# Pooled attention and MLP in one kernel: the first group's first product in blocks of 128 tokens, and the second group's loads in smaller pieces around the weights

One core of one Trainium2 chip runs the kernel. The metric is device time in microseconds (us) of that core, the median of several executions.

## The reference

```python
# q, k, v: (8, 8, 576, 64) f32;  moe_w_in: (512, 2048) f32;  moe_w_out: (2048, 512) f32
k_p = k.reshape(B, H, 72, 8, 64).mean(axis=3)          # pooling of 8 rows
v_p = v.reshape(B, H, 72, 8, 64).mean(axis=3)
attn = softmax(q @ k_p.transpose(0, 1, 3, 2) / 8)      # 576 x 72 for each head
x = (attn @ v_p).transpose(0, 2, 1, 3).reshape(4608, 512)
out = gelu_tanh(x @ moe_w_in) @ moe_w_out              # 4608 x 512, f32
```

## The kernel before

The kernel works on groups of 512 tokens. Groups 0 to 7 hold the first 512 tokens of each batch; a ninth group, R, holds the 64 tokens that are left of each, and is worked between groups 6 and 7. While TensorE does the MLP of one group, the other engines prepare the attention of the next one. Functions put into `hooks` at step s are called just before matmul s of the MLP, so the program order of every engine is written by hand.

For every group the normalised attention weights `eb` are transposed to `eT`. For group 0 TensorE does that; for all others the DMA does it (`e_transpose_dma`, four per group, issued from SyncE), and the values products, which start the next group, read `eT`.

```python
def e_transpose_dma(g, j):
    nc.sync.dma_start_transpose(out=st[g]["eT"][:, j], in_=eb[:, j])

def hidden_half(g, fo, half, hook, s):                 # first product of group 0: 256 tokens at a time
    c0 = 256 * half
    hp = psum.tile([128, 2, 256], F32, name="mm", tag="mm", bufs=4)
    for f in range(2):
        for ko in range(KO):
            hook(s + 4 * f + ko)
            nc.tensor.matmul(out=hp[:, f, :], lhsT=w_in_b[:, ko, (fo + f) * 128:(fo + f + 1) * 128],
                             rhs=st[g]["xT"][:, ko, c0:c0 + 256], start=(ko == 0), stop=(ko == KO - 1))
    nc.scalar.activation(out=gT[:, fo:fo + 2, c0:c0 + 256], in_=hp, func=ACT.Gelu_apprx_tanh)
# ... cut
def warm_up(n, tag):                                   # called with 12, ahead of the work
    warm = psum.tile([128, MAIN], F32, name="warm", tag=tag, bufs=BUFS[tag])
    for _ in range(n):
        nc.tensor.matmul(out=warm, lhsT=zeros, rhs=zeros.unsqueeze(1).to_broadcast([128, 4, 128]),
                         start=True, stop=True)
# ... cut: the loads of group 0 and of w_in stand ahead of these, all on SyncE's queue
load_main(1, "k", 0, 4, nc.sync)
load_half(1, "k", nc.sync)
load_half(1, "v", nc.sync)
load_q(1, 0, 4, nc.sync)
for c in range(4):
    w_out_load(c)                                      # 1 MB each
load_main(1, "v", 0, 2, nc.sync)
load_main(1, "v", 2, 4, nc.sync)
# ... cut: hooks of group 1's attention in group 0's MLP (second product from step 128 on)
for j in range(4):
    at(hooks, [128, 131, 142, 146][j], scores, 1, j)
    at(hooks, [128, 131, 142, 146][j], exps, 1, j)
    at(hooks, [142, 146, 150, 154][j], norm, 1, j, nc.vector)
    at(hooks, [142, 146, 150, 154][j], e_transpose_dma, 1, j)
for f in range(8, 16, 2):
    at(hooks, 147, cast_w_out, f, f + 2, nc.scalar)
# ... cut
tail_of_attention(hooks, 1, 186)                       # values of group 1
```

The softmax here doesn't subtract the row's maximum and nothing guards it: scores larger than these inputs give would overflow.

## Time and profile before

| | before |
|---|---|
| device time, median of 3 (lowest to highest) | 294.52 us (294.45 to 294.75) |
| span in the profile | 292.6 us |
| TensorE busy | 97% |
| first hidden matmul of group 0 | 17.43 us |
| first output matmul of group 0 | 35.71 us |
| values of group 1, start and end | 49.07 and 50.86 us |
| transposes of `eT` for group 1 landed | 46.44, 47.01, 47.58, 48.18 us |

The span is the profiled execution from its first to its last instruction; the device time is about 2 us longer. The lines of the page, of the stretches, of TensorE's timeline and of the chain stand in the prediction below.

### The profile page before, as it was taken

Reading aid. Unit: us, or ns where it says so; the run is one execution under the profiler, and the core shown is the slowest. Engines: PE = TensorE matmul, PEld = TensorE weight load, DVE = VectorE, ACT = ScalarE, POOL = GpSimd, SP = SyncE. Lnnn points to the kernel's source line nnn. Section 1 sums busy time; section 2 is a strip of 40 time slices with the busy share of each in tenths; the row PEclk is TensorE's granted clock in tenths of the full one; section 3 lists DMA queues with packets and bytes.
Section 4 is the critical chain, followed back from the end, with each engine's and each line's share of the span. In section 5 each row is a group of like instructions: output and inputs, shape, how many; then the busy total and the mean of one; then the engine's idle time right before and its main releaser. Section 6 shows DMA issues by size and latency. Waiting matters only on the chain.

```text
span 292.6 us, 4562 instructions
## 1 busy us (share of the span) xinstructions
PE 284.2 (97%) x1712; PEld 142.8 (49%) x1739; DVE 141.8 (48%) x236; ACT 156.4 (53%) x233; POOL 64.7 (22%) x86
## 2 busy tenths in 40 slices
PE   8899999999999999999999999999999999999996
PEld 3678753445444544454445444544444544444444
DVE  5892778076517460757065806481639100920012
ACT  1586574777067706671567257724673377436500
POOL 4575443222303040114002400240024000100000
PEclk9999999999999999999999999999999999999999
DMA  7999999996699369945994599148944900451012
GB/s 234 354 386 347 380 381 201 340 257 168 149 298 278 102 134 288 251 142 133 268 283 150 126 250 299 15 113 243 293 146 103 183 23 2 85 112 38 0 72 72
DMA packets 73301, 56.32 MB, mean 192 GB/s; under 512 B 45888, under 2 KB 55488, under 8 KB 73280
## 3 DMA queue, kind: packets, MB, share of 16 engines
q1 hardware_dynamic: 73136, 55.98, 69.6%
q8 instruction: 13, 0.21, 0.3%
q10 hardware_dynamic: 144, 0.07, 0.1%
q14 instruction: 8, 0.07, 0.1%
HBM read 36.70 MB, written 9.44 MB: 158 GB/s over the span
## 4 chain that ended last, share of the span: by engine, by line
PE 81%; DMA 8%; DVE 4%; SPq 3%; ACT 1%; issue 1%; POOL 0%; ACTq 0%
PE mm L360 37%; PE mm L344 36%; DMA w_out_s<-in_moe_w_out_dram 5%; DMA w_in_s<-in_moe_w_in_dram 3%; PE xo L310 3%; PE sc L214 2%; SPq L437 2%; DVE eb L248 1%; ACT gT L346 1%; PE mm L388 1%; DVE den L236 1%; SPq L99 1%; PE xo L319 1%; DVE kv L132 0%; DVE kv L133 0%
## 5 line engine op out<-in xcount | busy, mean ns | idle before, releaser
L360 PE MATMUL mm<-w_out_b,gT 128*128 128x512 bf16 x543 | 125.9, 379 | 1.4 <-issue 0.8
L344 PE MATMUL mm<-xT,w_in_b 128*128 128x512 bf16 x502 | 111.4, 379 | 0.5
L346 ACT ACTIVATE gT<-mm 128x512 bf16<-128x512 f32 x128 | 76.4, 597 | 38.4 <-PE mm L344 38.4
L360 PEld LDWEIGHTS <-gT 128*128 128x128 bf16 x560 | 53.1, 98 | 60.3 <-issue 3.1
L344 PEld LDWEIGHTS <-w_in_b 128*128 128x128 bf16 x512 | 50.1, 98 | 60.5 <-issue 0.3
L81 DVE COPY osb<-mm 128x512 f32<-128x512 f32 (+2 forms) x37 | 24.2, 657 | 58.9 <-PE mm L360 52.8
L79 ACT CAST xT<-xo 128x1024 bf16<-128x1024 f32 (+1 forms) x18 | 16.6, 967 | 56.6 <-PE xo L310 48.2
L154 POOL TENSOR_TENSOR vbd<-kvb,vmask 128x256 bf16<-128x256 bf16 (+2 forms) x40 | 21.5, 561 | 105.1 <-DVE kvb L134 104.9
L236 DVE TENSOR_REDUCE den<-e 128x8 f32<-128x576 f32 x36 | 26.5, 736 | 36.8 <-ACT e L229 36.8
L132 DVE TENSOR_TENSOR kv<-kv 128x1024 f32<-128x1024 f32 (+3 forms) x19 | 21.8, 1149 | 38.4 <-DMA kv<-in_v_dram 32.3
L229 ACT ACTIVATE e<-sc 128x576 f32<-128x576 f32 x36 | 22.4, 650 | 9.6 <-ACT e L229 4.1
L248 DVE TENSOR_TENSOR eb<-e,r 128x576 bf16<-128x576 f32 x24 | 23.3, 972 | 0.8
L81 POOL CAST q_b<-q_sb 128x2048 bf16<-128x2048 f32 (+2 forms) x9 | 17.4, 1937 | 14.5 <-DMA q_sb<-in_q_dram 14.5
L248 POOL TENSOR_TENSOR eb<-e,r 128x576 bf16<-128x576 f32 x6 | 6.9, 1150 | 57.3 <-ACT e L229 30.4
L355 PE MATMUL mm<-xT,w_in_b 128*128 128x256 bf16 x128 | 15.5, 273 | 0.2 <-DVE xT L81 0.2
L214 PE MATMUL sc<-kbd,qT 128*128 128x144 bf16 x128 | 13.3, 226 | 0.4 <-ACT qT L79 0.2
L214 PEld LDWEIGHTS <-qT 128*128 128x128 bf16 x128 | 9.9, 98 | 7.3 <-issue 0.7
L355 PEld LDWEIGHTS <-w_in_b 128*128 128x128 bf16 x128 | 12.1, 98 | 1.8 <-issue 0.3
L133 DVE TENSOR_TENSOR kv<-kv 128x512 f32<-128x512 f32 (+3 forms) x19 | 12.4, 651 | 0.7
L357 ACT ACTIVATE gT<-mm 128x512 bf16<-128x512 f32 x16 | 9.5, 597 | 5.9 <-PE mm L355 5.8
L558 ACT ACT_TABLE_LOAD x8 | 10.3, 1283 | 0.1
L81 POOL CAST w_in_b<-w_in_s 128x512 bf16<-128x512 f32 (+1 forms) x10 | 8.6, 874 | 2.4 <-DMA w_in_s<-in_moe_w_in_dram 2.4
(62 smaller groups left out, 123.5 us busy)
## 6 DMA issues: line engine op xcount, KB each, us to landing
out_dram<-osb SPq DMA_DIRECT2D x31, 256.0 KB, 6.8
kv<-in_k_dram SPq DMA_DIRECT2D x7, 1024.0 KB, 7.6
q_sb<-in_q_dram SPq DMA_DIRECT2D x7, 1024.0 KB, 6.2
kv<-in_v_dram SPq DMA_DIRECT2D x6, 1024.0 KB, 9.2
w_in_s<-in_moe_w_in_dram SPq DMA_DIRECT2D x8, 512.0 KB, 9.8
w_out_s<-in_moe_w_out_dram SPq DMA_DIRECT2D x4, 1024.0 KB, 13.7
kv<-in_v_dram SPq DMA_DIRECT2D x4, 512.0 KB, 10.2
out_dram<-osb SPq DMA_DIRECT2D x9, 128.0 KB, 2.4
```

The costliest lines, as they stand in the source:

```text
L79: eng.copy(out=out, in_=in_)
L81: eng.tensor_copy(out=out, in_=in_)
L132: add(out=t[:, :, 0:4, :], in0=t[:, :, 0:4, :], in1=t[:, :, 4:8, :], op=ALU.add)
L154: eng.tensor_tensor(out=vbd[p0:128, b, n0:n1, :].rearrange("p (c r) (hh d) -> p c (r hh) d", c=max(m, 1), d=D), in0=kvb[p0:128, 4 + c0:4 + ...
L214: nc.tensor.matmul(out=o, lhsT=qT[:, j, pr, :], rhs=kbd[:, g, pr].rearrange("d hh s -> d (hh s)"), start=True, stop=True)
L229: nc.scalar.activation(out=e.rearrange("p (x h) s -> p x (h s)", x=2), in_=sc[:, :, 0:4 * Sp], func=ACT.Exp, scale=1.0 / 64.0)
L236: nc.vector.reduce_sum(out=den, in_=e, axis=AX.X)
L248: eng.tensor_tensor(out=o.rearrange("p (h s) -> p h s", s=Sp), in0=e, in1=r.unsqueeze(2).to_broadcast([128, H, Sp]), op=ALU.mult)
L344: nc.tensor.matmul(out=hp, lhsT=w_in_b[:, ko, fo * 128:(fo + 1) * 128], rhs=st[g]["xT"][:, ko, :], start=(i == 0), stop=(i == KO - 1))
L346: nc.scalar.activation(out=gT[:, fo, :], in_=hp, func=ACT.Gelu_apprx_tanh)
L355: nc.tensor.matmul(out=hp[:, f, :], lhsT=w_in_b[:, ko, (fo + f) * 128:(fo + f + 1) * 128], rhs=st[g]["xT"][:, ko, c0:c0 + 256], start=(ko ...
L360: nc.tensor.matmul(out=o, lhsT=gT[:, fo, r * 128:(r + 1) * 128], rhs=w_out_b[:, fo, :], start=(fo == 0), stop=(fo == FO - 1))
```

## The change

The intent is to start TensorE's dense work earlier. Block 0 of 128 tokens can enter the first product as soon as its own attention is done; more weights are then used per token, so w_in is needed in another order. The loads of group 1 are cut into smaller pieces and moved around the weights: half of k goes ahead of w_in's last quarter, q comes in two loads, w_out's first MB in two, and half of v goes ahead of w_out's last MB. Two of the four norms of group 1 give three heads to ScalarE.

```diff
-    def hidden_half(g, fo, half, hook, s):
+    def hidden_block(g, c, j, hook, s):
-        hp = psum.tile([128, 2, 256], F32, name="mm", tag="mm", bufs=4)
-        for f in range(2):
+        hp = psum.tile([128, 4, 128], F32, name="mm", tag="mm", bufs=4)
+        for f in range(4):
+            fo = 4 * c + f
             for ko in range(KO):
...
-        for half, c in [(0, 0), (0, 1), (0, 2), (1, 0), (0, 3), (1, 1), (1, 2), (1, 3)]:
-            for fo in range(4 * c, 4 * c + 4, 2):
-                hidden_half(g, fo, half, hook, s)
-                s += 8
+        for c, j in [(0, 0), (0, 1), (1, 0), (1, 1), (0, 2), (1, 2), (0, 3), (1, 3)] + [(c, j) for c in (2, 3) for j in range(4)]:
+            hidden_block(g, c, j, hook, s)
+            s += 16
...   (w_in's loads)
+        if c == 3:
+            kv_tile(1)
+            load_main(1, "k", 0, 2, nc.sync)
...   (w_out's loads)
+        step = 2 if c == 0 else 4
+        for f in range(4 * c, 4 * c + 4, step):
...
-    load_main(1, "k", 0, 4, nc.sync)
+    load_main(1, "k", 2, 4, nc.sync)
     load_half(1, "k", nc.sync)
     load_half(1, "v", nc.sync)
-    load_q(1, 0, 4, nc.sync)
+    load_q(1, 0, 2, nc.sync)
+    load_q(1, 2, 4, nc.sync)
     for c in range(4):
+        if c == 3:
+            load_main(1, "v", 0, 2, nc.sync)
         w_out_load(c)
-    load_main(1, "v", 0, 2, nc.sync)
     load_main(1, "v", 2, 4, nc.sync)
...   (hooks of group 1; the second product now starts at step 256)
+    for f in range(8, 12, 2):
+        at(hooks, 275, cast_w_out, f, f + 2, nc.scalar)
+    for j in range(2):
+        at(hooks, 275, norm, 1, j, nc.vector)
+        at(hooks, 275, e_transpose_dma, 1, j)
+    at(hooks, 276, norm_two, 1, 2, 5)
+    at(hooks, 276, e_transpose_dma, 1, 2)
+    at(hooks, 277, cast_w_out, 12, 13, nc.scalar)
+    at(hooks, 277, norm_two, 1, 3, 5)
+    at(hooks, 277, e_transpose_dma, 1, 3)
+    for f0, f1 in [(13, 14), (14, 16)]:
+        at(hooks, 278, cast_w_out, f0, f1, nc.scalar)
```

Cut from the diff: `values_half` becomes `values_block` in the same way, the attention of group 0 is put in another order, and the remaining hooks move to the new step numbers.

## The prediction

> **What bounds the kernel now.** I read the page first, then busy time by stretches, then the timeline of TensorE from 14 to 53 us, and last the chain of waits up to 52 us. The page:
>
> ```profile
> span 292.6 us, 4562 instructions
> PE 284.2 (97%) x1712; PEld 142.8 (49%) x1739; DVE 141.8 (48%) x236; ACT 156.4 (53%) x233; POOL 64.7 (22%) x86
> PE   8899999999999999999999999999999999999996
> DMA  7999999996699369945994599148944900451012
> ```
>
> TensorE is busy 97% of the span at full clock; only the first two slices (15 us) are below 9 tenths. DMA is full from about 2 to 45 us and has room after that. By stretches (start of the first MLP product, start and end of what follows until the values of group 1 are done):
>
> ```profile
> 0.00:17.43 17.43, 14.43 (x100) 9.05 (x101) 12.65 (x26) 7.79 (x17) 8.79 (x23) 1.00 0.96 309
> 17.43:35.71 18.28, 17.71 (x171) 14.92 (x171) 11.62 (x25) 11.82 (x20) 9.61 (x12) 1.00 1.06 368
> 35.71:50.86 15.15, 14.97 (x85) 6.86 (x87) 11.65 (x20) 9.32 (x12) 6.96 (x9) 1.00 1.03 294
> 50.86:292.61 241.75, 237.06 (x1358) 112.00 (x1382) 105.85 (x166) 127.51 (x187) 39.31 (x44) 1.00 0.63 164
> ```
>
> Columns: stretch, length, busy time of PE, PEld, DVE, ACT, POOL, clock, DMA share, GB/s. The last row, 241.75 us, is seven and a half groups of dense matmuls that the diff leaves alone. All that can move is in the first 50.86 us. TensorE there:
>
> ```profile
> 16.81 0.41 PE L214 MATMUL sc<-kbd,qT 128*128 128x144 bf16 x4
> 17.43 1.91 PE L355 MATMUL mm<-xT,w_in_b 128*128 128x256 bf16 x16 [0.21 <-DVE xT L81]
> 19.75 1.47 PE L355 MATMUL mm<-xT,w_in_b 128*128 128x256 bf16 x12
> 23.06 9.01 PE L355 MATMUL mm<-xT,w_in_b 128*128 128x256 bf16 x81
> 49.07 1.79 PE L310 MATMUL xo<-eT,vbd 32*64 32x512 bf16 x16
> ```
>
> The first hidden product waits for the values' copy (DVE xT). From 23.06 on it runs solid. The values of group 1 take 1.79 us, where the same 16 take 1.18 us at 259 us: 0.6 us of waiting. The chain of waits says what stands behind both ends:
>
> ```profile
> 11.40 9.91 DMA w_in_s<-in_moe_w_in_dram
> 21.31 13.68 DMA w_out_s<-in_moe_w_out_dram
> 35.04 0.63 POOL w_out_b L81
> 45.45 0.61 DVE kv L132
> 48.88 0.62 POOL vbd L154
> 49.55 1.31 PE xo L310 x13
> ```
>
> The start of the second product hangs on w_out's first MB, which lands at 34.99 us. The end of the stretch hangs on VectorE (the norms of group 1 from 37.94, then the pooling of v) and GpSimd's spread. So the stage is bound by three things that lie within a microsecond of one another: TensorE's work, the order of the loads, and VectorE's chain. That is the reason to expect little.
>
> **What the Trainium skill says.** (1) "TensorE: Matmul & The Clock Gate", Back-to-back issue gap, gives about 81 ns for a 128-column matmul with its own weight load in a stream, against some 56 ns isolated. This decides what blocks of 128 cost, and the trace disagrees with 81: the 81 matmuls at 23.06 give (9.01-0.27)/80 = 109.2 ns for 256 columns; the last product has 16 of 256 and 32 of 128 columns in 3.55 us of the chain, so (3.55-16*0.1092)/32 = 56.3 ns; and 64 values of 64 columns, each with its own weight load, take 2.03 us, under 32 ns each. I use 56.3. (2) "SBUF — State Buffer", Who interferes with whom: a VectorE copy in two-port mode and GpSimd block each other for a whole instruction. The trace agrees: the same 512-element cast of w_in took VectorE 0.87 us while GpSimd was casting and 0.41 us without. (3) "DMA: Bandwidth & Descriptors", Why small descriptors are slow: a fixed cost per packet. The trace agrees: by its landings, 512 KB of v, in long rows, take 1.37 us (two loads, 8.65 to 11.40), and the halves of q, in 512-byte rows, 1.77 us (6.89 to 8.65 and 11.40 to 13.18); q of group 1 as one MB takes 2.75 us (29.55 to 32.30).
>
> **The change, part by part.**
> (a) Values and hidden in blocks of 128. The hidden matmuls go from 128 of 256 columns (128*109.2 = 13.98 us) to 256 of 128 (256*56.3 = 14.41): +0.43 us on TensorE, on the path. Values go from 16*109.2 = 1.75 to 32*56.3 = 1.80: nothing. The gelus stay 16 of 128x512. The copies of values become eight of half the size: off the path but for the first.
> (b) The start. Block 0 needs only the weights of token block 0. ScalarE loses the norm_two pieces of block 1 (3*0.28 us), so its copy of eT can start near 13.8 instead of 14.97. Values of block 0 then run at about 14.5 and, with the last spread of v near 15.2, at 15.3. Block 1's values stand before the hidden product in program order and need eT of block 1 (VectorE, near 15.9). w_in's first two loads land at 14.53 and 15.89 and their casts take 0.6 to 1.0 us, the second one behind the lock. So hidden starts near 16.8 instead of 17.43: -0.6 us.
> (c) What lies in the hidden stretch. Work after the change: 14.41 + scores of block 3 (0.25) + 10 transposes of e (0.57) + values of blocks 2 and 3 (16*0.0563 = 0.9) + transposes of k (0.28) and of q (16*0.057 = 0.91) = 17.3 us. Before: 13.98 + 0.57 + 0.87 + 0.28 + 0.91 = 16.6 us in 17.43 to 35.15, so 1.1 us idle. After the change the third block (quarter 1 of w_in) wants its weights near 19.1 and 19.6. The quarter's second half lands at 18.60, and before the casts behind it ended at 20.44; with less lock 19.9 to 20.4. I take 0.6 us of wait here. End of hidden: 16.8 + 17.3 + 0.6 = 34.7, against 35.15: -0.45 us.
> (d) The loads. Half of k (1.36 us) goes ahead of w_in's last quarter. It then lands near 26.6 instead of 25.2; it is wanted after 30, so free. w_out's first MB in two pieces: its first half would land 1.36 us before 34.99, but q in two loads of 512-byte rows costs 2*1.77-2.75 = +0.8 us ahead of it, so about 34.4. With a cast of 0.63 the second product can start at about 35.1 instead of 35.71: -0.6 us. The second half of q lands near 33.1 and its GpSimd cast (1.04 to 1.54 us) ends 34.2 to 34.6, just when its transposes are due: up to 0.4 us of wait, within the same limit of 35.1.
> (e) The end of the stretch. Norms of group 1: 2*1.7 + 2*1.47 (ScalarE takes three heads of two of them) instead of 4*1.7 = -0.46 us on the chain. Half of v ahead of w_out's last quarter lets its pooling start without waiting. But v's last half lands no earlier, since the same bytes stand ahead of it (45.74 before, about 46.5 with (d)), and the DMA transposes of e queue behind it: their last landing was 48.18, after it about 48.9. Pooling the last half ends near 48.0, spread to 48.7. So the values start near 49.0 and run without most of their 0.6 us of waiting: end near 50.2 instead of 50.86.
> Sum, at the end of the stretch: -0.6 us. After it nothing changes: 294.52 - 0.6 = **293.9 us**. The terms (b) and (d) don't add: each limit is passed in turn, and the last one, (e), sets what is left.
>
> **The rivals.** *One: narrow matmuls cost more than 56 ns* in a run of 256 beside a full DMA. At the skill's 81 ns, hidden would take 256*0.081 = 20.7 us, +6.8 us against 13.98, less the 0.6 of (b): about 300.5 us, slower by 2%. Against it: the 56.3 and 32 ns above. For it: those came late, when DMA was idle; but bursts of 8 transposes at 14.32, at full DMA, took 0.62 us, or 57 ns each without the 0.17 us of drain. I give this 3%. *Two: waits for w_in, q or w_out take the place of what is removed*, all of it: 294.5 to 295.3. For it: DMA is full until 44 us, the same bytes come in more pieces, and (c) lands on a cast. 25%. *Three: the loads don't pay for q's smaller rows, and VectorE with ScalarE lets the values start by 48.5*: then the start's 0.6, the shorter norms and the stall of the values all count, minus 0.4 for narrow matmuls: -1.3 to -1.7, 292.8 to 293.2. For it: the order of hooks was evidently placed to meet the loads. 20%.
>
> **Range and chances.** The middle case is 293.9. The range goes from rival three (292.8) to rival two with a bit more stall (295.3). Faster by 2% needs -5.9 us; all idle time of TensorE in the first 51 us is 17.43-14.43 + 18.28-17.71 + 15.15-14.97 = 3.8 us, so that is out of reach: 1%. Slower by 2% needs rival one: 3%. Within 2%: 96%.
>
> **What would show it.** Right: a 128-column hidden matmul every 56 ns in its long run; first hidden near 16.8; a gap near 19.5 to 20.3 before quarter 1's second half, released by GpSimd's w_in cast; the first output matmul near 35.1, released by the w_out cast; the group's values ending near 50.2; 241.7 us from there to the end. Wrong: a pitch well over 60 ns (rival one); first outputs at 35.7 or later or values after 50.9 (rival two); output from 34.5 or earlier and values done by 49.5 (rival three); any change of more than 0.5 us after the values of group 1, which I hold to be none.

## More of the kernel before

One line is in the page's list of DMA queues (packets, MB, share of the 16 engines' time):

```profile
q8 instruction: 13, 0.21, 0.3%
```

By the trace, each of these 13 packets has 16,384 bytes, and they come as TensorE works through its program. The Trainium skill, "Runtime: NRT & Kernel Launch", section Instruction fetch mechanics, explains them: instructions are streamed from memory in 16 KiB blocks of 256, by a DMA queue of the sequencer's own, and it says of the cost that it is "mostly hidden". The trace agrees with the block: on average 247 recorded TensorE instructions lie between two packets (187 to 292; a matmul counts as two, with its weight load, and some records are missing).

## The result and the profile after

The changed kernel takes 296.96 us (296.78 to 297.28) against 294.52, and both sit at full clock. The ratio is 1.0083, with a 95% interval of 1.0065 to 1.0100. Ratios here are the mean time of one kernel's fast runs over that of the other's in the same rounds, so they are not quite the ratio of the medians. Executions over 1.5% slower than the fastest of the same kernel are left out of the means. The result is correct. It is a small loss where a small gain was predicted (range 292.8 to 295.3 us).

The page of the kernel after, first line, busy times, and the queue of instruction fetches:

```profile
span 294.8 us, 4860 instructions
PE 284.2 (96%) x1856; PEld 145.2 (49%) x1883; DVE 142.0 (48%) x241; ACT 157.9 (54%) x240; POOL 65.1 (22%) x90
...
q8 instruction: 15, 0.25, 0.4%
```

TensorE is busy for the same 284.2 us; all of the 2.2 us are idle time. It has 144 more matmuls, and two more fetches. By stretches, with the same columns and the same borders as in the prediction:

```profile
0.00:16.57 16.57, 13.85 (x105) 8.87 (x105) 12.19 (x25) 7.23 (x15) 8.77 (x23) 1.00 0.95 306
16.57:35.38 18.81, 18.25 (x314) 17.47 (x312) 13.11 (x31) 11.87 (x22) 9.79 (x14) 1.00 1.07 343
35.38:52.33 16.95, 14.99 (x88) 6.71 (x88) 11.53 (x21) 11.33 (x19) 7.38 (x11) 1.00 1.11 291
52.33:294.83 242.50, 237.09 (x1357) 112.17 (x1382) 105.13 (x166) 127.48 (x187) 39.20 (x44) 1.00 0.63 165
```

The first stretch is 0.86 us shorter, as intended (16.57 against 17.43). The second gives 0.53 of that back. The third is 1.80 us longer, 16.95 against 15.15, with the same busy time. The last is 0.75 us longer, 242.50 against 241.75, although the diff touches nothing there. TensorE's timeline (start, length, what ran, and in brackets how long it had waited and for whom):

```profile
16.57 0.39 PE L355 MATMUL mm<-xT,w_in_b 128*128 128x128 bf16 x4
...
23.40 8.20 PE L355 MATMUL mm<-xT,w_in_b 128*128 128x128 bf16 x144
...
35.38 0.81 PE L360 MATMUL mm<-w_out_b,gT 128*128 128x512 bf16 x3
...
40.09 6.94 PE L360 MATMUL mm<-w_out_b,gT 128*128 128x512 bf16 x30
47.37 0.38 PE L360 MATMUL mm<-w_out_b,gT 128*128 128x512 bf16 x1 [0.34 <-ACT w_out_b L79]
48.32 1.89 PE L360 MATMUL mm<-w_out_b,gT 128*128 128x512 bf16 x8 [0.57 <-ACT w_out_b L79]
51.15 1.18 PE L310 MATMUL xo<-eT,vbd 32*64 32x512 bf16 x16 [0.94 <-DMA eT<-eb]
```

In the kernel before, the 39 output matmuls that here begin at 40.09 ran through without a wait:

```profile
40.34 8.80 PE L360 MATMUL mm<-w_out_b,gT 128*128 128x512 bf16 x39
```

So the sum for group 1, end of the values, can be taken from the two timelines. The 39 matmuls begin 0.25 us earlier. They take 1.32 us longer, from 40.09 to 50.21 = 10.12 us against 8.80, because they wait twice for ScalarE's cast of w_out (0.34 and 0.57, together 0.91); the other 0.41 us goes at the two restarts. Then TensorE waits 0.94 us for the DMA transposes; before, the values followed the matmuls at once (49.07 against 40.34 + 8.80 = 49.14, overlapping by 0.07), so this is +1.01. The values take 1.18 instead of 1.79 us, as predicted, which is -0.61. Together: -0.25 + 1.32 + 1.01 - 0.61 = +1.47 us, which is the 52.33 against 50.86.

The chain of waits of the kernel after, up to there (start, length, what):

```profile
32.46 12.96 DMA w_out_s<-in_moe_w_out_dram
...
45.97 0.84 ACT eb L266 x3
...
46.84 4.22 DMA eT<-eb
51.15 1.18 PE xo L310 x16
```

The chain runs from w_out's last MB, which lands at 45.42, through ScalarE (its cast stands ahead of the last three heads of block 3), to the last transpose, and that transpose takes 4.22 us to land. It no longer goes through VectorE and GpSimd. The transposes of group 1 landed at 47.43, 49.38, 50.62 and 51.06. Between the first two lie 1.95 us, where before there were 0.57. What the DMA engines did in the microsecond after 47.0 is in the DMA view of that window, in 40 slices of 0.025 us (GB/s of each, and the fetch):

```profile
GB/s 276 307 287 287 307 276 287 297 205 154 297 266 257 208 943 266 256 267 287 266 276 256 276 266 276 276 276 276 266 256 287 276 184 20 20 20 0 0 0 0
...
q8 instruction: 1, 0.02, 6.8%
```

A block of TensorE's instructions is fetched at 47.4 us (the slice with 943). Some 0.45 us later, at 47.83, the rate falls to nothing, with three transposes still to land, and stays there until about 49.0. The packets that start in the window from 47.75 to 49.00 take long (their time is 1.58 of the window on each of the 16 engines, the column before the last), and 20 GB/s are moved:

```profile
47.75:49.00 1.25, 0.68 (x4) 0.32 (x4) 1.01 (x3) 1.23 (x2) 0.56 (x2) 1.00 1.58 20
```

The same view of the kernel before, 44 to 49 us in slices of 0.125, has no fetch, and the data of its transposes move without a break from 45.6 (slice 14) to 47.6:

```profile
GB/s 170 121 88 82 66 82 51 84 51 51 37 35 115 265 291 293 295 256 267 285 291 283 242 228 256 231 207 219 138 33 0 0 25 25 16 0 16 16 41 131
```

Something of the same kind happens in group R. From the view of `eT` between 215 and 236 us, before:

```profile
DMA to landing us min/median/max: 2.5/2.6/2.6
```

and after, where a fetch comes at 226.2:

```profile
DMA to landing us min/median/max: 2.6/3.2/4.6
```

From the first product of group 6 to that of R are 31.00 us after (202.92 to 233.92) and 30.48 before (201.57 to 232.05): +0.52. From the first product of group 7 to the end are 31.07 against 30.73, +0.34. All groups between lie within 0.12 us of before. So 1.47 - 0.12 + 0.52 + 0.34 = 2.21 us, which is the difference of the spans.

Why does the fetch fall there? The change adds 128 + 16 matmuls to TensorE's program, with their weight loads 288 instructions. That is one block of 256 and 32 more, so every later fetch comes 32 instructions earlier, some 3.5 us in the output phase, where two instructions take 0.216 us (7 more matmuls in 1.89 - 0.38 us at 48.32). For the fetch beside group R's transposes the trace has it so: 226.21 - 202.92 = 23.29 us after the first product of group 6, against 228.14 - 201.57 = 26.57 before. I had counted the matmuls' time, and not their place in memory.

### The profile page after: what moved, and what is told of

Its sections match the earlier page's. It is cut to its first block, busy times and chain, and to the rows that moved or that the text cites. A ratio compares the mean times of both kernels' runs of the same rounds, so it can differ in the third digit from the quotient of the medians.

```text
span 294.8 us, 4860 instructions
## 1 busy us (share of the span) xinstructions
PE 284.2 (96%) x1856; PEld 145.2 (49%) x1883; DVE 142.0 (48%) x241; ACT 157.9 (54%) x240; POOL 65.1 (22%) x90
## 4 chain that ended last, share of the span: by engine, by line
PE 80%; DMA 13%; SPq 3%; ACT 2%; issue 1%; POOL 1%; DVE 0%; ACTq 0%; POOLq 0%
PE mm L344 36%; PE mm L360 36%; DMA w_out_s<-in_moe_w_out_dram 4%; DMA w_in_s<-in_moe_w_in_dram 4%; PE xo L310 3%; DMA kv<-in_v_dram 2%; DMA eT<-eb 2%; PE sc L214 2%; ACT gT L346 1%; PE mm L388 1%; SPq L454 1%; SPq L99 1%; POOL w_in_b L81 1%; PE vp L141 1%; PE xo L319 1%
## 5 line engine op out<-in xcount | busy, mean ns | idle before, releaser
L344 PEld LDWEIGHTS <-w_in_b 128*128 128x128 bf16 x512 | 50.1, 98 | 60.6 <-issue 0.3
L79 ACT CAST xT<-xo 128x1024 bf16<-128x1024 f32 (+1 forms) x21 | 17.3, 861 | 55.1 <-PE xo L310 46.6
L132 DVE TENSOR_TENSOR kv<-kv 128x512 f32<-128x512 f32 (+3 forms) x20 | 22.3, 1114 | 35.1 <-DMA kv<-in_v_dram 31.7
L81 POOL CAST q_b<-q_sb 128x2048 bf16<-128x2048 f32 (+2 forms) x9 | 16.5, 1833 | 15.5 <-DMA q_sb<-in_q_dram 15.5
L355 PE MATMUL mm<-xT,w_in_b 128*128 128x128 bf16 x256 | 16.4, 219 | 0.0
L355 PEld LDWEIGHTS <-w_in_b 128*128 128x128 bf16 x256 | 14.7, 98 | 0.3
L133 DVE TENSOR_TENSOR kv<-kv 128x256 f32<-128x256 f32 (+3 forms) x20 | 12.5, 626 | 0.7
```

The costliest lines, as they stand in the source:

```text
L79: eng.copy(out=out, in_=in_)
L81: eng.tensor_copy(out=out, in_=in_)
L132: add(out=t[:, :, 0:4, :], in0=t[:, :, 0:4, :], in1=t[:, :, 4:8, :], op=ALU.add)
L344: nc.tensor.matmul(out=hp, lhsT=w_in_b[:, ko, fo * 128:(fo + 1) * 128], rhs=st[g]["xT"][:, ko, :], start=(i == 0), stop=(i == KO - 1))
L355: nc.tensor.matmul(out=hp[:, f, :], lhsT=w_in_b[:, ko, fo * 128:(fo + 1) * 128], rhs=st[g]["xT"][:, ko, 128 * j:128 * j + 128], start=(ko ...
```

## The experiments

Three theories stand against each other. **Fetch (F):** the loss is made by the place of the instruction fetches among the DMA transposes, which a pure shift of the program would undo. **Loads (L):** the loss is made by the order and the pieces of the loads, which bring w_out's last MB and v's last half later. **Narrow matmuls (N):** 256 small ones cost time by themselves, in a way that the busy time does not show. The expectations may name the theories in other words.

### A first look, with four kernels

The first four were run on one chip (before: 294.93 us there). Two shift TensorE's program without touching anything else, by another form of the warm-up matmuls: about the same columns (6188 and 4992, against 6144) in more and narrower matmuls.

```diff
-    def warm_up(n, tag):
+    def warm_up(n, tag, c=512):
...
+            if c == 512:
...
+            else:
+                nc.tensor.matmul(out=warm[:, 0:c], lhsT=zeros, rhs=zeros[:, 0:c], start=True, stop=True)
...
-    warm_up(12, "mm")
+    warm_up(119, "mm", 52)      # s1, on the kernel after: +214 instructions
+    warm_up(39, "mm", 128)      # s2, on the kernel before: +54 instructions
```

> The changed kernel with nothing altered but its warm-up: 119 matmuls of 52 columns instead of 12 of 512 (about the same columns), so that every later TensorE instruction stands 214 places further back. Theory F (instruction fetch): the 16 KB block of TensorE instructions that was fetched at 47.4 us, in the middle of the four DMA transposes of e of group 1, is now fetched after about 52 us; the transposes land by about 49.5 instead of 51.06, the values of group 1 start at about 50.2 instead of 51.15, and the kernel takes 295.5 to 296.2 instead of 296.96. Theory L (order of loads and ScalarE's queue alone): nothing in the work, the loads or the queues has changed, so 296.8 to 297.1 and values at about 51.1.

Measured: 296.63 us, 1.0054 (1.0035 to 1.0074). The shift moved a fetch to 8.2 us, where the first loads of v were held up (the second landed at 11.26 instead of 9.91), and TensorE was at half clock from 12.6 to 16.0 us. The dense work started 2.6 us later than after. From TensorE's timeline:

```profile
19.15 0.39 PE L355 MATMUL mm<-xT,w_in_b 128*128 128x128 bf16 x4
...
53.21 2.03 PE L344 MATMUL mm<-xT,w_in_b 128*128 128x512 bf16 x8
```

Yet group 1's first product began at 53.21, earlier than the 53.57 of after: the last transpose landed at 50.34 instead of 51.06, with 0.57 us between the first two, and the values did not wait. Two things follow. The start of group 0 hardly sets the end of this stretch: 2.6 us later, TensorE came to the values only 0.5 us after the last transpose (42.01 + 8.85 = 50.86 by its timeline), so the 0.86 us won there are worth little by themselves. And with the fetch away from the transposes the wait for `eT` was gone. The expected time was missed by 0.4 us: in group 2 a wait for the keys had appeared, 0.61 us at 68.59, which after does not have (see k1 and the section on all traces).

> The kernel before with 39 warm-up matmuls of 128 columns instead of 12 of 512: later TensorE instructions stand 54 places further back. Theory F: its fetch of 52.3 us comes at about 46.5 us, in the middle of the transposes of e (45.5 to 48.2), which then land 1 to 1.5 us later; values of group 1 start 0.4 to 1.3 us later, and the kernel takes 294.9 to 296.0. Theory L: same as before, 294.3 to 294.8.

Measured: 295.01 us, 1.0000 (0.9985 to 1.0016). A fetch now came at 46.5 us, and the transposes of the kernel before landed at 46.72, 48.82, 49.38 and 49.94, the last one 1.76 us later than in before. So a fetch can delay the transposes with no other change. TensorE, itself 0.5 us later than in before (40.86 + 8.80 = 49.66), then waited for them:

```profile
50.08 1.18 PE L310 MATMUL xo<-eT,vbd 32*64 32x512 bf16 x16 [0.42 <-DMA eT<-eb]
```

The values then ran without their stall (1.18 us instead of 1.79), and group 1's first product began at 52.50 instead of 52.10. The median did not move. So the delay of the transposes and a wait of 0.42 us are shown; that they cost time as a whole is not, in the kernel before.

```diff
     for c in range(4):                                  # e1, on the kernel after
-        if c == 3:
-            load_main(1, "v", 0, 2, nc.sync)
         w_out_load(c)
+    load_main(1, "v", 0, 2, nc.sync)
     load_main(1, "v", 2, 4, nc.sync)
```

> The changed kernel with the last quarter of w_out loaded ahead of the first half of v again, as before. Theory L: w_out's quarter lands at about 44.0 instead of 45.42, ScalarE's cast of it no longer holds up its three heads of block 3, TensorE no longer waits for w_out (0.9 us at 47.4 and 48.3), the last transpose of e is issued near 45.3 instead of 46.84, and the kernel takes 295.3 to 296.0. Theory F: the fetch at 47.4 still falls among the transposes, so most of the loss stays: 296.4 to 297.

Measured: 297.95 us (296.46 to 299.12), 1.0095 (1.0070 to 1.0120). The edit did what it should at first: w_out's last MB landed at 44.19, and TensorE never waited for it. But the fetch still came at 47.4, the last transpose landed at 51.34, and TensorE, which was now early, stood idle for 2.37 us. One limit had taken the place of another. And the gap cost more than its length. The windows of this run from 50 us on (the column after the five busy times is the clock):

```profile
50.00:51.00 1.00, 0.00 (x0) 0.00 (x0) 0.25 (x1) 0.00 (x0) 0.10 (x1) 1.00 0.88 196
51.00:52.00 1.00, 0.57 (x8) 0.22 (x8) 0.00 (x0) 0.00 (x0) 0.00 (x0) 0.63 1.09 318
52.00:53.00 1.00, 1.00 (x16) 0.19 (x8) 0.00 (x0) 0.00 (x0) 0.00 (x0) 0.50 1.09 347
...
54.00:55.00 1.00, 1.00 (x5) 0.34 (x3) 0.50 (x1) 1.00 (x2) 0.53 (x1) 0.66 1.06 387
```

The granted clock fell to half for about 3.4 us. Four of the six executions had a mean clock of 0.994 and took 297.77 to 299.12 us; the two near full clock took 296.46 and 296.82. So the fall costs some 1.7 us when it comes (the means of the four and of the two are 298.36 and 296.64). The Trainium skill, "TensorE: Matmul & The Clock Gate", gives in its section What's actually happening a window of about 3.4 us for both directions, and advises in Why this matters for your kernels against gaps of more than some 3 us. The length of the low clock agrees; the safe gap does not, since here the fall came with a gap of 2.37 us.

```diff
     at(hooks, 276, e_transpose_dma, 1, 2)               # e2, on the kernel after
-    at(hooks, 277, cast_w_out, 12, 13, nc.scalar)
     at(hooks, 277, norm_two, 1, 3, 5)
     at(hooks, 277, e_transpose_dma, 1, 3)
+    at(hooks, 277, cast_w_out, 12, 13, nc.scalar)
```

> The changed kernel with ScalarE's three heads of block 3 ahead of its first cast of w_out's last quarter. Theory L: block 3 of e is ready near 45.0 instead of 46.81, its transpose is issued near 45.1; but TensorE still waits for w_out, even 0.5 us more if the cast is moved behind: values near 50.2 to 50.6, kernel 296.0 to 296.6. Theory F: with the transposes done earlier by 1.5 us less of them is left when the fetch comes at 47.4, so it would help too, to the same 296.0 to 296.6; only the landing times tell.

Measured: 297.17 us, 1.0080 (1.0057 to 1.0104). Block 3 was normalised earlier, but the last transpose was still issued at 46.79: SyncE was held in the issue of the third transpose from 44.27 on, for 2.41 us, to shortly before v's last half landed (46.95). So the order on ScalarE, which the chain of waits names, is not what holds the transposes. The expectation was wrong. TensorE waited 1.86 us for `eT`, and the clock fell to half here too, from 52.85 to 56.26.

### Work and loads taken apart

One chip again (before: 294.85 us).

```diff
-    warm_up(12, "mm")           # f1, on the kernel after: s2's shift of 54 instructions
+    warm_up(39, "mm", 128)
```

> The changed kernel with 39 warm-up matmuls of 128 columns instead of 12 of 512 (54 more TensorE instructions ahead, and none of the early trouble that the shift by 214 brought, where a fetch fell on the first loads of v). Theory F: the fetch of 47.4 us comes near 42, while w_out and v load; the last transpose of e lands at 49.4 to 49.9 instead of 51.06, the values of group 1 start at 50.2, the second group's first product at 52.6 instead of 53.57, and the time falls by about 1 us against the changed kernel (ratio to before 1.004 to 1.006). If the fetch alone is not it: ratio 1.008 as in the first comparison.

Measured: 296.32 us, 1.0044 (1.0028 to 1.0060). The fetch came at 43.8 us, ahead of the transposes, and they landed at 48.20, 48.76, 50.00 and 50.43. The view of `eT` from 38 to 53 us has these times from issue to landing, for after and then for f1:

```profile
DMA to landing us min/median/max: 4.2/6.9/7.3
```

```profile
DMA to landing us min/median/max: 2.8/5.7/7.1
```

TensorE did not wait for them (no bracket), in f1:

```profile
50.90 1.18 PE L310 MATMUL xo<-eT,vbd 32*64 32x512 bf16 x16
```

In group R the loss was gone too: 202.97 to 233.44 are 30.47 us, as in before. The loads came 0.8 us later (v's last half at 47.62), so not all of it arrived in the time. Nor is f1 a clean test: its first fetch came at 15.4 instead of 19.1 us, TensorE waited three times for casts of w_in (0.45, 0.62 and 0.46 us near 20 to 22) and began the 39 output matmuls at 41.20 instead of 40.09. That it did not wait for `eT` is in part its own lateness. And a fetch at 134.8 now fell among the transposes of group 4; TensorE waited 0.23 us for them, and from the first product of group 3 to that of group 4 were 30.14 us instead of 29.84.

> The changed kernel's blocks and hooks with the loads of the kernel before (k, q and w_out's first MB in one piece each, v last). Theory L says the loads bring the loss: v's last half lands at 45.8 instead of 46.86, w_out's last quarter at 43.2, the TensorE waits for w_out go; ratio to before 1.000 to 1.004, with the fetch at 47.4 still among the transposes. Theory B (the blocks bring it, by their 288 TensorE instructions that move the fetch): ratio 1.004 to 1.008, transposes last landing 49.5 to 50.

g1 is the kernel after with all loads as before. Measured: 296.81 us, 1.0060 (1.0038 to 1.0083). v's last half landed at 45.94, but a fetch at 46.5 put 1.91 us between the first two transposes, and the last landed at 50.39. In addition TensorE waited 1.56 us at 34.08, since k was still pooled in the pieces of the new loads while it came in one. TensorE was so late by this that the values did not wait for `eT`. So the old loads alone do not mend it.

> The kernel before with only its loads in the new order and pieces. Theory L: v's last half lands at 46.6 to 46.9 instead of 45.74 and w_out's last quarter at 45.4 instead of 43.10; the last transpose lands at 49.0 to 49.4 instead of 48.18; values start 0.3 to 0.8 us later; ratio 1.001 to 1.004. Theory B: no change, within 0.1%.

g2 is the kernel before with all loads as after. Measured: 296.40 us, 1.0046 (1.0029 to 1.0063), and no fetch near the transposes (last landing 48.54). So the new loads cost by themselves, with the old work order. That is in favour of L as a part of the cause, but in the trace only 0.33 us of it lie in the stretch that the loads touch (group 1's first product at 52.43 instead of 52.10); 0.77 of the other 0.88 us lie between the first products of groups 4 and 6, with waits of 0.32 and 0.18 us for keys, and are not explained.

```diff
-        at(hooks, [142, 146, 150, 154][j], norm, 1, j, nc.vector)          # h1, on the kernel before
-        at(hooks, [142, 146, 150, 154][j], e_transpose_dma, 1, j)
-    for f in range(8, 16, 2):
+    for f in range(8, 12, 2):
+        at(hooks, 147, cast_w_out, f, f + 2, nc.scalar)
+    for j in range(4):
+        if j < 2:
+            at(hooks, 147, norm, 1, j, nc.vector)
+        else:
+            at(hooks, 147, norm_two, 1, j, 5)
+        at(hooks, 147, e_transpose_dma, 1, j)
+    for f in range(12, 16, 2):
```

> An attempt to beat both: the kernel before, with blocks 2 and 3 of group 1 normed by VectorE and ScalarE together and ScalarE's casts of w_out's last quarter behind them. VectorE is free near 44.7 instead of 45.4, pools v's last half from 45.8, GpSimd's spread ends near 48.6 instead of 49.85, and the values of group 1 no longer stall (0.6 us): ratio 0.997 to 0.999. If the transposes or TensorE's own work set the end there: 1.000.

Measured: 294.65 us, 0.9994 (0.9977 to 1.0012). Group 1's first product began at 51.70 instead of 52.10, but the time did not follow beyond the noise.

### Fewer or more narrow matmuls

One chip (before: 294.88 us), with the kernel after once more as a control.

> The changed kernel unaltered, as a measure for the others on this chip: ratio to before 1.006 to 1.009, values of group 1 at about 51.1.

Measured: 297.57 us, 1.0093 (1.0075 to 1.0111). The loss repeats, with the fetch at 48.1 and 1.94 us between the first two transposes.

```diff
-                nc.tensor.matmul(out=hp[:, f, :], ..., rhs=st[g]["xT"][:, ko, c0:c0 + 256], ...)     # i1, on before
+            for y in range(2):
+                    nc.tensor.matmul(out=hp[:, f, 128 * y:128 * y + 128], ...,
+                                     rhs=st[g]["xT"][:, ko, c0 + 128 * y:c0 + 128 * y + 128], ...)
```

> The kernel before, in which nothing but each 256-column hidden matmul is given as two of 128 columns: same loads, same waits, same order, 256 TensorE instructions more. TensorE's own work grows by 0.43 us. Theory F: a third instruction fetch comes before 45 us and a fourth near 46 to 47, the last transpose of e lands at 49.5 to 50 instead of 48.18, and the kernel takes 1.0 to 2.0 us more (ratio 1.0035 to 1.007). Theory L: only TensorE's 0.43 us, ratio 1.001 to 1.002.

Measured: 294.81 us, 1.0002 (0.9990 to 1.0014). 128 more matmuls of half the width cost nothing that can be measured, and neither does the one more fetch among the loads (at 30.2 and 36.6 us instead of 32.1). This rules N out, as far as the kernel before can show it. (In its trace the stretch is 1.1 us longer, with waits of 0.85 and 0.78 us for VectorE's norms of group 0; that execution, 295.32 us, was its slowest.) F's expectation failed for a plain reason that I had overlooked: 256 more instructions are a whole block, so the fetches after them stay where they were relative to the work.

```diff
+        for fo in range(8, FO):          # i2, on the kernel after: the last two quarters in 512 columns
+            hp = psum.tile([128, MAIN], F32, name="mm", tag="mm", bufs=4)
+            for ko in range(KO): ...
+                nc.tensor.matmul(out=hp, lhsT=w_in_b[:, ko, fo * 128:(fo + 1) * 128], rhs=st[g]["xT"][:, ko, :], ...)
```

> The changed kernel, with the last two quarters of the first product done in 512 columns (32 matmuls instead of 128; 192 TensorE instructions fewer, and 0.3 us less TensorE time). Theory F: no fetch between about 40 and 50 us, transposes land at 49.4 to 49.8, values start at 50.2, ratio 1.003 to 1.005. Theory L: only the 0.3 us: ratio 1.006 to 1.008.

Measured: 295.41 us, 1.0030 (1.0017 to 1.0043), 2.16 us under the control of the same chip. 192 instructions less put the fetches at 41.9 and 70.0 us, and the transposes landed at 47.43, 48.00, 49.23 and 49.66. TensorE's timeline has the values without a wait for `eT`, 1.01 us earlier than in after:

```profile
50.14 1.18 PE L310 MATMUL xo<-eT,vbd 32*64 32x512 bf16 x16
```

Group R took 30.47 us again. The waits for w_out stayed (0.40 and 0.57 us). In this stretch i2 and after differ in the fetch and in little else: v's last half landed at 46.86 in both, the last transpose was issued at 46.84 in both, and TensorE was through with its output matmuls at 48.33 + 1.89 = 50.22 against 50.21. So the 1.01 us are not the saved work.

```diff
     (i2, and)                            # j1
-    load_q(1, 0, 2, nc.sync)
-    load_q(1, 2, 4, nc.sync)
+    load_q(1, 0, 4, nc.sync)
     for c in range(4):
-        if c == 3:
-            load_main(1, "v", 0, 2, nc.sync)
         w_out_load(c)
+    load_main(1, "v", 0, 2, nc.sync)
```

> All the undoings at once, as an attempt to keep the early start without its costs: the same in 512 columns, q of group 1 in one load, and w_out's last quarter ahead of v. v's last half at 46.0, transposes done at 48.5 to 48.9, values start at 49.0 and don't stall; ratio 0.998 to 1.001 if fetches and loads are the whole loss. If it stays over 1.004, something else in the change costs.

Measured: 294.64 us, 1.0000 (0.9988 to 1.0013), 2.93 us under the control. With the fetch out of the way and two of the load edits undone, the whole loss is gone, with blocks of 128 in half of the first product and the rest of the change in place. Nothing is won either; its second product begins at 36.19, later than before's 35.71, after waits for k and q (0.43 and 0.68 us). TensorE now reaches the values at 49.55 without a wait, but v's last half lands at 46.54, 0.8 us later than in before, and the values stall inside again (1.68 us):

```profile
49.55 1.68 PE L310 MATMUL xo<-eT,vbd 32*64 32x512 bf16 x16
```

### The fetch moved in steps

If F holds, the time must depend on where the fetch falls and not on how much work is narrow. k1 does two of the sixteen rows of the first product in 512 columns (48 instructions less), k2 ten rows with four warm-ups less (248 less, so that the fetch comes back among the transposes). Same edit as i2 with other numbers. On this chip the times scattered more (before: 294.32 to 296.98 us, median 295.09).

> The changed kernel with only the last two of 16 rows of the first product in 512 columns: 48 TensorE instructions fewer, under 0.1 us less TensorE time. Theory F: the fetch of 47.4 us moves to about 52.5, behind the transposes, and the one of 226.2 to about 231, behind those of the last group; transposes land by 49.8, the values start at 50.2; ratio 1.003 to 1.005. If the number of narrow matmuls counts: ratio 1.007 to 1.009, hardly changed.

Measured: 297.18 us (295.57 to 298.04), 1.0063 (1.0031 to 1.0096). The fetch moved from 47.4 to 55.45, the transposes landed 0.57 us apart (last at 50.50), the values did not wait, and the last group took 30.48 us. All this is as F has it, and still the time is not. In the profile a new wait of 1.25 us appeared in group 2, for the keys: group 2's k landed at 59.83 us instead of 58.04. The fetch had moved among the loads of group 2, and the section on all traces shows what that does. Another group had 30.47 us where the others have 29.84.

> The changed kernel with ten of 16 rows of the first product in 512 columns and four warm-up matmuls fewer: 248 TensorE instructions fewer, nearly a whole block of 256. Theory F: a fetch comes near 46.5 us again, among the transposes, which land at 50 to 51, so that this kernel, with the least work of all its kind, is slower than the one with eight rows (1.0030): ratio 1.005 to 1.008. If the number counts: ratio 1.002 to 1.003, the best of the series.

Measured: 296.70 us, 1.0052 (1.0025 to 1.0079). The fetch came at 47.2, there were 2.12 us between the first two transposes, and the values waited 0.97 us, although this kernel has fewer narrow matmuls than i2. Both stood at 1.0052 and 1.0030, so the order is as F says, but on two sets of rounds with overlapping intervals.

```diff
-    load_q(1, 0, 2, nc.sync)             # d1, on the kernel after
-    load_q(1, 2, 4, nc.sync)
+    load_q(1, 0, 4, nc.sync)
```

> The changed kernel with q of group 1 in one load. v's last half lands at 46.2 instead of 46.86 (0.7 us less), but the fetch at 47.4 still falls among the transposes: ratio 1.006 to 1.008. If the loads were the main cause: 1.003 to 1.005.

Measured: 296.21 us, 1.0033 (1.0005 to 1.0061). Better than expected, though in its profile the fetch is still among the transposes (2.00 us between the first two, values waiting 1.00 us) and group 1's first product starts at 53.83, no earlier than after's. Group R took 30.57 us instead of 31.00; the rest of the gain in the median the profile doesn't show, and with this interval I take it as unresolved.

```diff
-        t = w_out_s[c // 2][...]         # h2: h1, and w_out's first MB in two loads
+        step = 2 if c == 0 else 4
+        for f in range(4 * c, 4 * c + 4, step): ...
```

> Attempt to beat the kernel before: its own code with norms of blocks 2 and 3 shared by VectorE and ScalarE, and w_out's first MB in two pieces, so that the second product starts at 35.4 instead of 35.71. Ratio 0.997 to 0.999; 1.000 if the transposes behind the loads (48.2 to 48.7) set the end of the stretch.

Measured: 294.51 us, 0.9984 (0.9953 to 1.0015). Not faster than before by anything the rounds can tell. It was the attempt at a version that beats both.

### A last pure shift

> The changed kernel with 76 warm-up matmuls of 84 columns instead of 12 of 512 (128 TensorE instructions, half a block, ahead), nothing else. Theory F: no fetch between about 36 and 57 us, transposes of group 1 done by 49.5 to 50.4, no wait for them; none in the last group either; 1.0 to 2.0 us less than the unaltered changed kernel in this job. If the place of the fetch does not matter: within 0.5 us of it.

z1 is the kernel after with 76 warm-ups of 84 columns, +128 instructions. Measured: 297.17 us, 1.0083 (1.0063 to 1.0102) from five fast runs of 296.1 to 298.1 us. This is a miss for F, which expected one to two us less. Three of the five had a mean clock of 0.987 to 0.994, so a part of it may be a low clock at the start, as in s1. Its profile fell into an execution of 768 us, so its trace is not compared with anything and can't say where the fetches fell.

> The changed kernel unaltered, as the measure for the other: ratio to before 1.007 to 1.010, a fetch near 47.4 among the transposes.

z2 is the kernel after once more. Measured: 297.21 us, 1.0093 (1.0078 to 1.0107), at full clock in all runs. So the loss of the kernel after has been measured three times, on at least two chips: 1.0083, 1.0093, 1.0093.

### What all traces say together

This table has every usable trace, with the landings of group 1's four transposes and the fetch nearest to them.

| kernel | fetch near 44 to 51 us | landings, us | first to second |
|---|---|---|---|
| after | 47.4 | 47.43 49.38 50.62 51.06 | 1.95 |
| a0 (after again) | 48.1 | 48.18 50.12 51.37 51.81 | 1.94 |
| z2 (after again) | 47.5 | 47.61 49.55 50.79 51.23 | 1.94 |
| d1 | 47.5 | 47.66 49.65 50.83 51.28 | 2.00 |
| e1 | 47.4 | 47.54 49.49 50.74 51.34 | 1.95 |
| e2 | 47.4 | 47.52 49.47 50.73 51.33 | 1.95 |
| k2 | 47.2 | 47.33 49.45 50.53 51.00 | 2.12 |
| g1 | 46.5 | 46.67 48.57 49.87 50.39 | 1.91 |
| s2 (before, shifted) | 46.5 | 46.72 48.82 49.38 49.94 | 2.10 |
| before | none | 46.44 47.01 47.58 48.18 | 0.57 |
| i1 (before, split) | none | 46.65 47.20 47.71 49.14 | 0.56 |
| h1, h2 (before, norms) | none | 46.49 47.05 48.22 48.69; 46.61 47.20 48.38 48.82 | 0.56; 0.59 |
| g2 (before, new loads) | none | 46.71 47.29 47.85 48.54 | 0.58 |
| f1 (after, shifted) | 43.8 | 48.20 48.76 50.00 50.43 | 0.57 |
| i2 (after, wide) | none | 47.43 48.00 49.23 49.66 | 0.57 |
| j1 (i2, old loads of q and v) | none | 47.12 47.69 48.89 49.35 | 0.57 |
| k1 (after, two rows wide) | none | 48.28 48.84 50.07 50.50 | 0.57 |
| s1 (after, shifted) | none | 48.11 48.67 49.91 50.34 | 0.57 |

In nine of nine traces with a fetch within the 0.3 us before the first landing, the second transpose comes 1.91 to 2.12 us after the first; in ten of ten without, it comes after 0.56 to 0.59 us. The condition was brought about in both kernels and taken away in four ways. So it is shown that a fetch in this place goes with a stall of some 1.4 us of the transposes. What in the DMA engines makes it stall, no run shows.

The same 19 traces show two things more. First, the later groups: of their 532 transposes, 489 took 2.55 to 2.72 us from issue to landing. The other 43 took 2.82 to 4.60, and all of them stand in a group with a fetch among its four transposes or within half a microsecond before one. In before, one of group 2 took 4.10 us (issued at 70.69, fetch at 70.96) and TensorE did not wait for it. So a stalled transpose costs time only where TensorE has no slack. Second, plain loads: from the landing of group 2's q to that of its k passed 4.31 to 4.91 us in the seven traces with a fetch between 52.2 and 55.5 us, and 2.94 to 3.31 in the twelve without. The pure shifts show it in both directions (s1 4.43 against 3.15 in after, s2 3.08 against 4.33 in before). That is the wait for keys in k1 and s1, where the fetch had been moved away from the transposes. Not every load was held up: w_out's came 2.7 us apart with a fetch at 32.1 (before) or at 36.6 (i1) as without.

## Why the prediction was right or wrong

**(a) Narrow matmuls: right.** The run of 144 took 8.20 us, so (8.20 - 0.22)/143 = 55.8 ns each, where 56.3 was used. The skill's 81 ns would have been wrong, and rival one with it; i1 confirms it in time (1.0002).

**(b) The start: right in time, wrong in worth.** 16.57 us against the predicted 16.8. But s1, which started 2.6 us later, had group 1 ready 0.36 us earlier. What ends the stretch in after is the stream of loads and the transposes behind it, which the start doesn't touch. Nor was the start still ahead when the hidden product ended, as (c) shows.

**(c) and (d) Hidden and the loads: half right.** The hidden product gave way to the last scores at 35.14 (predicted 34.7, before 35.16), so nothing of the early start was left there, and the first output was at 35.38 (predicted 35.1, before 35.71). The sum in (c) was too small: it has 16.6 us of work and 1.1 us idle before, where its own row has 17.71 of 18.28 us busy; after, 18.25 of 18.81 us were busy, where it has 17.3 us of work. The wait for w_in did not come (0.19 us near 19.1, for VectorE's norm); the one for q, 0.37 us at 34.23 behind GpSimd's cast, was foreseen. w_out's first half landed at 34.30 (34.4), and q in two loads took 32.98 - 29.75 = 3.23 us instead of 32.30 - 29.55 = 2.75, so 0.48 us more (0.8). What (d) left out is a consequence of its own order: with half of v ahead, w_out's last MB lands at 45.42 instead of 43.10, and TensorE then waits for its casts: 1.32 us. That is a wait of the kind that rival two describes, at a place that it did not name. j1 against i2, where this and q's split are undone, gave -0.77 us in the medians. Two readings of the profile were wrong without consequence: the cast of 0.41 us was not without GpSimd, whose own cast of w_in began with it at 17.30 and took 1.32 us instead of 1.04; and the row of 241.75 us holds eight groups, not seven and a half.

**(e) The end of the stretch: this is the step that failed.** "the DMA transposes of e queue behind it: their last landing was 48.18, after it about 48.9", and from that "the values start near 49.0". v's last half landed about as predicted (46.86 against 46.5). The last transpose landed at 51.06 and the values started at 51.15. The step took the time from load to transposes as given. Two terms were missing in its sum: the fetch of instructions, 1.95 - 0.57 = 1.38 us on the transposes, and the waits for w_out on TensorE, 1.32 us. They overlap: without the fetch the last transpose would have landed near 51.06 - 1.38 = 49.68, an estimate, and TensorE itself arrived at 50.21. So the fetch cost about 0.94 us at the values, and i2, with the fetch elsewhere and the waits for w_out in place, had its last transpose at 49.66 and started them at 50.14. So even without the fetch the predicted 48.9 was 0.8 us too early. The gain of (e), values that run without a stall, was real: 1.18 us instead of 1.79.

**"After it nothing changes": wrong, by 0.74 us.** The same work has its fetches at other places there. In group R the second transpose is held up by one (4.56 us) and TensorE waits; the time from group 6 to R is 0.52 us longer. This depends on the moment: it was 30.47 or 30.48 us in f1, i2 and j1, where the fetch held up the first transpose, and in k1, where it came earlier; but also in e2 and k2, where it held up the second as in after. The 0.34 us at the end go with a fetch at 290.7 us. A store that is issued some 4 us before the end landed 2.99 us later, and in before 1.86. In all nine traces with a fetch in the last 5.1 us this store took 2.70 to 3.25 us, in the other ten 1.82 to 1.94; group 7 to the end took 30.89 to 31.25 us in the nine and 30.66 to 30.89 in the ten. No run was made to test it.

What is shown and what stays open: the mechanism in the traces (nine against ten) and the waits for w_out are shown. In time, the reading is carried by i2 and j1 against the control on the same chip (-2.16 and -2.93 us), and f1 fits it in part. z1 does not, and k1 and s1 show that a moved fetch can cost elsewhere, at group 2's keys. The control of i2 and j1 (297.57) was the slowest of the three measurements of after; by the profiled spans i2 is 1.60 us below the first one (293.24 against 294.83). No shift left the start of the kernel alone, so how much of the 2.4 us belongs to the fetch by itself is known only from the sum of the two timelines: some 0.94 + 0.52 us, and perhaps the 0.34 at the end. Low clock is not a part of the loss of the kernel after, whose four runs were all at full clock, but it made e1, e2, s1 and perhaps z1 harder to read.

## What to carry to other kernels

A change in the number of TensorE's instructions moves all its later instruction fetches; if DMA transposes or loads are on the path, look at the queue of instruction fetches in the DMA view, ask what each fetch will fall on at its new place too, and when an unrelated stage changes by half a microsecond, look there first. An earlier start is worth nothing when the stretch is ended by a stream of loads and what queues behind it: ask first what ends it. When a load is moved ahead of another, follow the one that was moved back to whoever waits for it.

## What the Trainium skill lacked or had wrong

- "Runtime: NRT & Kernel Launch", Instruction fetch mechanics: the cost of a block boundary is called mostly hidden. It was among the loads of q and w_out (one more fetch in i1: 1.0002, 0.9990 to 1.0014), but a fetch just ahead of queued DMA transposes went with 1.91 to 2.12 us between two landings instead of 0.56 to 0.59, in nine traces of nine, and a fetch among group 2's loads with 4.31 to 4.91 us from q to k instead of 2.94 to 3.31.
- "DMA: Bandwidth & Descriptors", DMA Transpose (X-bar): it has no word on a transpose beside an instruction fetch. Here transposes of 128x640 in bf16 landed 0.57 us apart from a queue and took 2.55 to 2.72 us alone, but up to 4.60 us with a fetch.
- "TensorE: Matmul & The Clock Gate", Back-to-back issue gap: about 81 ns for a 128-column matmul with its weight load in a stream; here 55.8 ns over 144 of them, which is what the section gives for an isolated one.
- The same page, Why this matters for your kernels, advises against idle gaps of more than about 3 us; here half clock for 3.4 us came with a gap of 2.37 us (e1, some 1.7 us of loss) and one of 1.86 us (e2), and not with 1.56 us (g1).
